# A Fourier filter gated by a ReGLU network: seven block products for a pair of feature tiles in the first 512 rows, four roots by iteration, first turns in halves, and a new order of the program

## The chip, the cores and the metric

The kernel runs on one core of a Trainium2 chip. A core has a matrix engine (TensorE, PE in the profile; its weight loads are listed apart as PEld), a vector engine (VectorE, DVE), a scalar engine for functions of one argument (ScalarE, ACT), a third elementwise engine (GpSimd, POOL), and an engine that here only starts transfers (SyncE, SP). They work at the same time, each on its own queue of instructions in order, and wait for one another by semaphores. The metric is the device time of one run in microseconds. Lower is better.

## The reference

For an input `x` of 2048 rows and 512 columns in 32-bit floats:

```
xn = (x - mean) / sqrt(var + 1e-5)              # each row
X  = rfft2(xn) * (w_r + 1j * w_i)               # over both axes
s  = irfft2(X, (2048, 512))
gate = xn @ W_gate                              # 512 x 1376
up   = xn @ W_up
h    = where(gate > 0, gate, 0) * up
g    = silu(h @ W_down)                         # 1376 x 512
out  = x + s * g
```

So two long chains start from the same normalized rows, a two-dimensional Fourier filter and a gated network, and they meet in the last line.

## The kernel before

**Numbers.** TensorE multiplies 16-bit floats with 32-bit sums. To keep the accuracy each 32-bit matrix is split into a high and a low 16-bit part, and each product is made of three: high by high, high by low, low by high (`PASSES`). Before such a split the weights are scaled by powers of two.

**Rows and features.** The 2048 rows are eight chunks of 256, or four blocks `c` = 0 to 3 of 512 rows, which are four row tiles of 128. The 1376 features are eleven feature tiles `f` = 0 to 10, of which the last has 96. For one block, one feature tile and one of the two matrices a plain product (`product`) is 12 matmuls of 512 columns: four pieces of the 512 input columns, three passes each. Then `rectify` (ScalarE) and `hidden` (VectorE, ScalarE) make the hidden tile `h`; `down` multiplies it by W_down, three matmuls for each feature tile and row tile; `gate` applies silu on ScalarE to the sum of a row tile.

**Seven block products.** For two feature tiles (a pair of `PAIRS`) `fast_products` takes another way, in the manner of Strassen and Winograd: instead of the four plain products of the pair it makes seven block products of 12 matmuls of 256 columns, into the tiles `sa`, `sb` and `sc`, and puts them together with copies and sums on ScalarE and VectorE (`sk`, `se`, `sr`, `sq`). It needs sums and differences of the rows, made by `row_sums` (`sx` on VectorE, ScalarE and POOL, written to memory as `S_d` and read back transposed as `xS`), and sums and differences of the weights, made by `weight_sums` once for each pair (`rp`, `wT`). `fast(c, n)` says whether block `c` uses it for pair `n`: `c >= 4 - int(FASTS[n])`. With `FASTS` at '3' for all five pairs, block 0 makes plain products everywhere and blocks 1 to 3 use the seven products in all pairs.

**The start.** The first 256 rows are loaded, normalized in two tiles `xf`, and turned on TensorE (`turn_row`: `head`, then the copy `xTf` in 32 bits and the 16-bit parts in `xT0`). While the split weights aren't ready, the first two feature tiles are multiplied in 32 bits from `xTf` for the first 256 rows (the matmuls `gu<-xTf,raw`, eight steps of four). Other chunks are turned through memory by SP.

**The normalization of later rows.** `deviations` handles chunks 2 and 3 together, and chunks 4 to 7 together: variance plus epsilon and its reciprocal on VectorE, the square root on ScalarE (line 412), one multiplication on VectorE. The square root and silu are in different function tables of ScalarE, which loads one when it changes from the other. So the silu gates of block 0 read the name "roots", which both calls of `deviations` write (line 961 and after), and come after all square roots.

**The filter.** `first_stage`, `fft_chunk` (eight chunks of frequencies, tiles `xx`, `y`, `z`, `v`, `w`) and `last_stage` (eight chunks of rows, TensorE tile `s`, then `zz`, `ae`, `ye`, `sv`) do the transforms as matmuls with constant matrices. The matmuls of some of these stages run on a part of TensorE's array, a mode of tiling that differs from that of the other products; the last feature tile's narrow product (`gu<-xT,wgt 128*64`) has a mode of its own too.

**The end.** `finish` multiplies the filter's rows by the gate (`sv<-sv,g`) and adds `x`: for chunks 0, 1, 3, 4 and 5 by a transfer on POOL's queue that accumulates onto `x` already copied to the output, for the others by a sum on an engine (`xt<-xt,sv`) and a plain transfer on SP. The last row tile of all is cut into pieces of 256, 128 and 128 columns (`columns`; TensorE's tiles `dn`, `dn_3b`, `dn_3bb`), so that the work behind TensorE's last matmul is short.

**The order.** The program doesn't run its loops as they stand. Each function lists steps in a `Plan` (class at line 176): an engine, what it reads and writes, and a function that makes its instructions. `run` then makes the steps in the sequence `ORDER` (line 68), a tuple of 1606 step numbers; each engine keeps the sequence of its own steps. A step that may run on either of two engines takes the letter in `PLACE` (D, A or P for VectorE, ScalarE or POOL), and a tile takes its buffer from `SLOTS`. So the order of work on every queue is written out by hand, and all instructions carry the line of one helper, L169. Tiles are to be told apart by their names.

Of the kernel before, what the change touches and what calls it, by code (L numbers as in the profile page):

```python
# [15 lines left out]
P = 128  # L16
# [31 lines left out]
BUSY, LATE = 28, 0.4  # L48
SQUARES, HALF = 63.305, 2
# [14 lines left out]
FASTS = ['3', '3', '3', '3', '3']  # L64
# [63 lines left out]
)  # L128
PLACE = (
    "AAPAADAADDAAADADDDADDDAPPDPDDDADDDPDDPAAADAADDDDDPPDPDDDDDDDDDDDDDDPPDADDDAAAADAAADDADDDDPDDDDDDDDDDDDDDDDDDDDPDDDDDDDPPDPPPDPADDDDDDPDDDDDD"  # L130
    "DDDDDDDDDDDDDPDPDDDDDPDDDDDPDPPPDDPDPDDPPPDDDDDPPDPDPPDPDDDDDDPDDDPDDDDDDDDDDDPPDPDDDDPPPDDDDDPPPDDDDPPPDDDPDPDDDDDDDDDDDDDDDDDDDDDDDDDDDDDD"
    "DDDDDDDDDDDDDDDDDDDDDDDDDDDDDDDDDDDDDDDDDDDDDDDDDDDDD"
)
SLOTS = (
# [104 lines left out]
def dve(n):  # L239
    return .07 + n / 960  # L240
# [27 lines left out]
def kernel(ctx: ExitStack, tc: tile.TileContext, x, wg, wu, wd, wl, ew, sp, c_r, c_d, c_m, c_x, c_s, out):  # L268
# [227 lines left out]
    def turn_row(c, i):  # L496
# [6 lines left out]
        elif i == 0:  # L503
            tile_of(name, "F", [P, 2, D], F32)
# [960 lines left out]
```

## Time and profile before

| what | value |
|---|---|
| median of 3 runs | 388.28 us (387.56 to 388.38) |
| the profiled run | 387.25 us, its span 385.4 us |
| TensorE (PE) | 378.9 us busy, 98% of the span, 3525 matmuls |
| VectorE (DVE) | 308.3 us, 80% |
| ScalarE (ACT) | 254.3 us, 66% |
| GpSimd (POOL) | 73.0 us, 19% |
| transfers | 77.95 MB, 202 GB/s on the mean |
| mean granted clock of TensorE | 0.998 of full speed |

The span is the time from the first to the last event of the program in the profile; the run's own time is a little longer. Records of one engine overlap: a matmul of 256 columns has a record of 0.273 us, but twelve of them in a row take 1.31 us. Where a duration of a row of work is wanted, the starts of neighbouring records say more than the mean record. The share of the span in which each engine was busy, in forty slices, in tenths (9 is 90% or more):

```profile
PE   8999999999999999999999999999999999999995
DVE  4999999989769999995369875687368872499996
ACT  4999999899955954666476645664565744386321
POOL 3200102000041200413502132322023033102220
```

TensorE is at 9 in all slices but the first and the last. VectorE is at 9 in the first fifth, in the middle and at the end; ScalarE only in the first quarter.

### The profile page before, as it was taken

How to read it: one execution, taken by the hardware profiler on the slowest of the kernel's cores; microseconds unless marked ns; L12 is line 12 of the kernel's file. 1: busy time of each engine (PE TensorE's matmuls, PEld its weight loads, DVE VectorE, ACT ScalarE, POOL GpSimd, SP SyncE). 2: the span in 40 equal slices, each digit the busy share in tenths (PEclk: the TensorE clock that was granted, in tenths of full speed). 3: DMA queues.
4: the chain of work that ended last, by engine and by line, in shares of the span. 5: the costliest groups of instructions: out<-in, count | busy, mean ns of one | idle time of the engine just before them, and what ended most of it. 6: DMA issues, size and time to landing. Idle time of an engine off the chain costs nothing.

```text
span 385.4 us, 8914 instructions
## 1 busy us (share of the span) xinstructions
PE 378.9 (98%) x3525; PEld 261.7 (68%) x3525; DVE 308.3 (80%) x560; ACT 254.3 (66%) x494; POOL 73.0 (19%) x72
## 2 busy tenths in 40 slices
PE   8999999999999999999999999999999999999995
PEld 6955444444778877646888788755588788778444
DVE  4999999989769999995369875687368872499996
ACT  4999999899955954666476645664565744386321
POOL 3200102000041200413502132322023033102220
PEclk9999999999999999999999999999999999999999
DMA  7989799795369386978858165482676027998997
GB/s 249 404 261 364 206 195 262 229 278 153 109 176 257 115 281 215 261 162 226 269 184 224 60 176 131 107 243 55 196 206 192 2 54 201 225 239 244 226 267 188
DMA packets 67833, 77.95 MB, mean 202 GB/s; under 512 B 29072, under 2 KB 40944, under 8 KB 67792
## 3 DMA queue, kind: packets, MB, share of 16 engines
q1 hardware_dynamic: 66352, 74.77, 67.8%
q0 software_dynamic: 1440, 2.62, 4.4%
q8 instruction: 27, 0.44, 0.5%
q14 instruction: 14, 0.11, 0.1%
HBM read 46.95 MB, written 26.76 MB: 191 GB/s over the span
## 4 chain that ended last, share of the span: by engine, by line
PE 90%; ACT 4%; DVE 3%; DMA 2%; issue 0%; POOL 0%; DVEq 0%
PE dn L169 25%; PE gu L169 17%; PE sb L169 15%; PE sc L169 10%; PE sa L169 10%; PE s L169 3%; PE z L169 3%; PE xx L169 3%; DMA x<-in_x 2%; PE y L169 2%; PE v L169 2%; ACT ju L169 2%; ACT wds L169 1%; DVE xT L169 1%; ACT wT L169 1%; PE dn_3b L169 0%
## 5 line engine op out<-in xcount | busy, mean ns | idle before, releaser
L169 PE MATMUL dn<-wds,h 128*128 128x512 f16 (+2 forms) x528 | 118.9, 372 | 0.0
L169 PEld LDWEIGHTS <-wgu 128*128 128x128 f16 x960 | 92.7, 98 | 36.4 <-issue 1.9
L169 PEld LDWEIGHTS <-h 128*128 128x128 f16 (+1 forms) x594 | 54.4, 98 | 51.4 <-issue 1.8
L169 PEld LDWEIGHTS <-wT 128*128 128x128 f16 x540 | 52.5, 98 | 8.6 <-issue 0.4
L169 PE MATMUL gu<-xT,wgu 128*128 128x512 f16 (+1 forms) x240 | 47.5, 358 | 0.0
L169 PE MATMUL sa<-xT,wgu 128*128 128x256 f16 x360 | 44.3, 273 | 0.0
L169 PE MATMUL sb<-xS,wT 128*128 128x256 f16 x360 | 44.2, 273 | 0.0
L169 PE MATMUL sc<-xS,wgu 128*128 128x256 f16 x180 | 22.1, 273 | 0.2 <-ACT g L169 0.2
L169 PE MATMUL sb<-xS,wgu 128*128 128x256 f16 x180 | 22.1, 273 | 0.0
L169 PE MATMUL sc<-xT,wT 128*128 128x256 f16 x180 | 22.1, 273 | 0.0
L169 DVE TENSOR_TENSOR sc<-sb,sk 128x512 f32<-128x512 f32 x15 | 10.4, 696 | 12.2 <-PE sb L169 9.1
L169 ACT ACTIVATE g<-dn,cdi 128x512 f32<-128x512 f32 (+1 forms) x16 | 10.4, 671 | 11.5 <-PE dn L169 11.5
L169 DVE TENSOR_TENSOR t<-v,t 128x1024 f16<-128x1024 f32 x8 | 9.8, 1222 | 9.4 <-ACT t L169 9.2
L169 POOL TENSOR_TENSOR se<-se,sq 128x512 f32<-128x512 f32 x9 | 11.5, 1273 | 30.2 <-ACT sq L169 30.2
L169 PE MATMUL gu<-xT,wgt 128*64 128x256 f16 (+1 forms) x144 | 17.0, 309 | 0.0
L169 ACT ACTIVATE sq<-sc 128x512 f32<-128x512 f32 x15 | 9.0, 597 | 12.0 <-PE sc L169 7.3
L169 DVE TENSOR_TENSOR h<-gu,r 128x512 f32<-128x512 f32 (+3 forms) x22 | 12.5, 566 | 4.4 <-ACT r L169 2.4
L169 ACT ACTIVATE sb<-sa 128x512 f32<-128x512 f32 x15 | 8.8, 587 | 9.7 <-PE sa L169 8.2
L169 ACT ACTIVATE t<-v 128x1024 f16<-128x1024 f32 x8 | 8.2, 1023 | 10.5 <-PE v L169 10.5
L169 DVE TENSOR_TENSOR w<-xsp,w 128x1024 f32<-128x1024 f32 (+1 forms) x13 | 13.5, 1041 | 1.7 <-ACT w L169 1.3
L169 POOL DMA_DIRECT2D out<-sv x10 | 8.8, 895 | 31.5 <-DVE sv L169 29.3
L169 DVE TENSOR_TENSOR sr<-sb,sr 128x512 f32<-128x512 f32 x15 | 10.3, 685 | 5.4 <-POOL se L169 2.7
(216 smaller groups left out, 721.0 us busy)
## 6 DMA issues: line engine op xcount, KB each, us to landing
rw<-in_wl SPq DMA_DIRECT2D x8, 512.0 KB, 5.5
A_d<-t SPq DMA_DIRECT2D x16, 256.0 KB, 3.5
wt<-in_wl SPq DMA_DIRECT2D x8, 512.0 KB, 5.6
at<-A_d SPq DMA_DIRECT2D x8, 512.0 KB, 5.7
C_d<-t SPq DMA_DIRECT2D x16, 256.0 KB, 3.3
ct<-C_d SPq DMA_DIRECT2D x16, 256.0 KB, 8.1
xf<-in_x SPq DMA_DIRECT2D x6, 512.0 KB, 4.9
N_d<-xf SPq DMA_DIRECT2D x6, 512.0 KB, 3.4
```

Source lines behind the costliest of these rows:

```text
L169: return lambda *args, **kw: self.tc.keep_in_program_order(f(*args, **kw))
```

## The change

1. `FASTS[1]` becomes '4': the pair (3, 4) takes the seven block products in block 0 too. For that `row_sums(0)` runs (two more writes and two more transposed reads on SP), and `weight_sums` of that pair runs before block 0's products. Its plain products, `rectify` and `hidden` of block 0 go.
2. `ITERATE = (4,)`: for chunks 4 to 7 the inverse root is made on VectorE from a first guess by integer arithmetic on the bits and three steps of Newton's iteration, 12 small instructions. The square root on ScalarE goes there, and with it the write of "roots". Chunks 2 and 3 stay as they were.
3. The turns of the first chunk (`head0_0`, `head0_1`), their copies `xTf` and the 32-bit products are done in halves: two transposes, 256 columns, and two matmuls at a time. A `head0` tile is now twice as large, one half for each.
4. `ORDER` (1635 steps), `PLACE` and `SLOTS` are new throughout. Counting the steps, TensorE has 441 (428 before), VectorE 464 (460), ScalarE 434 (426), SP 230 (226) and POOL 66 (66). At the end, the three pieces of the last row tile come in another sequence on TensorE, the 256-wide one last; and `PLACE` gives the last sum of the program (`xt`, that piece's) to POOL.

```diff
+ITERATE = (4,)
...
-FASTS = ['3', '3', '3', '3', '3']
+FASTS = ['3', '4', '3', '3', '3']
...
 ORDER = (
...
 PLACE = (
...
 SLOTS = (
...
-        step("DVE", .38, run, reads=[(st, 2, c, i) for c in cs for i in range(2)], writes=[(q, 0)], port=True)
-        step("ACT", .2, lambda: ACT.activation(y(), v(), AF.Sqrt), reads=[(q, 0)], writes=[(q, 1), "roots"])
-        step("DVE", .19, lambda: DVE.tensor_mul(w(), T[st][:, 1, :], y()), reads=[(q, 1), *((st, 1, c) for c in cs)], writes=[(q, 2)], port=True)
+
+        def iterate():
+            b = T[q].bitcast(I32)
+            DVE.tensor_scalar(w(), T[st][:, 2, :], 64.0 / (D * XS ** 2), EPS * 64.0 / XS ** 2, op0=ALU.mult, op1=ALU.add)
+            DVE.tensor_scalar(b[:, 1, :], b[:, 0, :], -0.5, float(0x5F3759DF), op0=ALU.mult, op1=ALU.add)
+            for k in range(3):
+                DVE.scalar_tensor_tensor(v(), y(), -(4.0 ** -k), y(), op0=ALU.mult, op1=ALU.mult)
+                DVE.tensor_mul(v(), v(), w())
+                DVE.scalar_tensor_tensor(y(), v(), 3.0, y(), op0=ALU.add, op1=ALU.mult)
+            DVE.tensor_mul(w(), T[st][:, 1, :], y())
+        sums_of = [(st, 2, c, i) for c in cs for i in range(2)]
+        if cs[0] in ITERATE:
+            step("DVE", 1.9, iterate, reads=sums_of, writes=[(q, 2)], port=True)
+        else:
...
-        if c == 0:
-            tile_of(name, "F", [P, D], F32)
-        elif i == 0:
+        if c == 0 or i == 0:
             tile_of(name, "F", [P, 2, D], F32)
...
+            def part(a):
+                for k in range(2):
+                    PE.transpose(T[name][:, a, k * P:k * P + P], T[f"xf{c}"][:, i, (2 * a + k) * P:(2 * a + k + 1) * P], unit)
+            for a in range(2):
+                step("PE", .22, lambda a=a: part(a), reads=[(f"xf{c}", i)], writes=[(name, a)], due=HEADS[c])
+            for a in range(2):
+                to = lambda a=a: T[n][:, 2 * a:2 * a + 2].rearrange("p k r -> p (k r)")
+                half = lambda a=a: T[name][:, a, 0:256]
+                T.either([("DVE", dve(256), ...), ("ACT", act(256), ...)], reads=[(name, a)], writes=[(n, a)])
...
-            def whole(j):
-                for k in range(4):
+            def whole(j, a):
+                for k in range(2 * a, 2 * a + 2):
                     matmul(to()[:, j], T[f"raw{g}_{i}"][:, k, :], T[f"xTf{j}"][:, k, :], start=k == 0, stop=k == 3)
...
-            if k > 1 and k % 2 and any(fast(k // 2, n) for n in range(len(PAIRS))):
+            if k % 2 and any(fast(k // 2, n) for n in range(len(PAIRS))):
                 row_sums(k // 2)
...
+    quick = [n for n in range(len(PAIRS)) if fast(0, n)]
     for f in range(HALF, NFT):
+        if any(f in PAIRS[n] for n in quick):
+            continue
...
+    for n in quick:
+        weight_sums(n, TDUE[n])
+        fast_products(0, n)
```

More of the change, by code (lines that the diff above doesn't have):

```diff
@@ L68 @@
 ORDER = (
[59 rows of a table removed]
[61 rows of a table added]
 )
 PLACE = (
-    "AAPAADAADDAAADADDDADDDAPPDPDDDADDDPDDPAAADAADDDDDPPDPDDDDDDDDDDDDDDPPDADDDAAAADAAADDADDDDPDDDDDDDDDDDDDDDDDDDDPDDDDDDDPPDPPPDPADDDDDDPDDDDDD"
-    "DDDDDDDDDDDDDPDPDDDDDPDDDDDPDPPPDDPDPDDPPPDDDDDPPDPDPPDPDDDDDDPDDDPDDDDDDDDDDDPPDPDDDDPPPDDDDDPPPDDDDPPPDDDPDPDDDDDDDDDDDDDDDDDDDDDDDDDDDDDD"
-    "DDDDDDDDDDDDDDDDDDDDDDDDDDDDDDDDDDDDDDDDDDDDDDDDDDDDD"
+    "DDADAAADDADAADAADADDDAAAAPPDDDDDDPDDDDADDDDPPDDAAAAADDADDDDDDDDDDDDDDPADDDDPPDADADDAADAAAADDADDDDPPDDDPDDDDDDDDDDDDDPPADDDDDDDPDPDPDDDADDPPD"
+    "PDDDDDDDDDDDDDDDDDPDDPPDDDDPDDDDDDDDDDDDDPDDDDDPPDPDDDDDPDDDPPDPPPDDDDDPDPDDDDDDDDDDDDDPDPPPDDDDPPPDDDPDDDDDDPPPPPDDDPDPDDDDDDDDDDDDDDDPDDDD"
+    "DDDDDDDPDDDDDDDDDDDPDDDDDDDDDDDDDDDDDDDDDDDDDDDDDDDDDDDDDPDDDD"
 )
 SLOTS = (
-    "00003891323300007162135011720253014206000044921016491487006302918390831448196549051670311501506699616223562219980241411630961259022411185122"
-    "118355963087666020137021820014270591614a0712616053172020422112237076505040213939265842321003128002102303401201206a00210210270213103150709201"
-    "061020130218321031320221002101402011301a52011012791676006052512023100810220121a2102123370012301354021203196074222100050105031418612308120017"
-    "18100661041017212507040603141111190500083508110706021759321618242005037420040717191107751215040608131956031118309032000430614165211041514364"
-    "908398707619212758514201652630376734"
+    "00003891320320000170131631610452056113200075191932782816815130071419574100068800714490180233151055252084185619817646017504695800967422649560"
+    "65194719064917776404002140a25015239070451312820016130712306305324702121037400120307476547162012301a01202102970213203580021101316102302123046"
+    "461704250123210590123201120123103700012313268201230234151a301022610220131521023027620123023902011203022101320a415081130206201016101933251807"
+    "00212311012901171108040806603506072922111920311005141815095637080302041112297811142620011654270611151309057089020761672650522701137130812040"
+    "4434919559808212310057573261064734355407"
 )
@@ L410, in run @@
             DVE.reciprocal(v(), w())
-        step("DVE", .38, run, reads=[(st, 2, c, i) for c in cs for i in range(2)], writes=[(q, 0)], port=True)
-        step("ACT", .2, lambda: ACT.activation(y(), v(), AF.Sqrt), reads=[(q, 0)], writes=[(q, 1), "roots"])
-        step("DVE", .19, lambda: DVE.tensor_mul(w(), T[st][:, 1, :], y()), reads=[(q, 1), *((st, 1, c) for c in cs)], writes=[(q, 2)], port=True)
+        def iterate():
[11 more added lines that the diff above has]
+        else:
+            step("DVE", .38, run, reads=sums_of, writes=[(q, 0)], port=True)
+            step("ACT", .2, lambda: ACT.activation(y(), v(), AF.Sqrt), reads=[(q, 0)], writes=[(q, 1), "roots"])
+            step("DVE", .19, lambda: DVE.tensor_mul(w(), T[st][:, 1, :], y()), reads=[(q, 1), *((st, 1, c) for c in cs)], writes=[(q, 2)], port=True)
         for j, c in enumerate(cs):
@@ L500, in turn_row @@
         name = f"head{c}" + f"_{i}" * (c == 0)
-        if c == 0:
-            tile_of(name, "F", [P, D], F32)
-        elif i == 0:
+        if c == 0 or i == 0:
             tile_of(name, "F", [P, 2, D], F32)
         j = 2 * (c % 2) + i
-        head = lambda: T[name] if c == 0 else T[name][:, i, :]
+        head = lambda: T[name][:, i, :]
         xt = lambda h: T[f"xT{c // 2}"][:, j, 4 * h:4 * h + 4].rearrange("p k r -> p (k r)")
@@ L512, in run @@
                 PE.transpose(head()[:, cols], T[f"xf{c}"][:, i, cols], unit)
-        step("PE", .45, run, reads=[(f"xf{c}", i)], writes=[(name, i)], due=HEADS[c])
-        if c == 0:
+        if c:
+            step("PE", .45, run, reads=[(f"xf{c}", i)], writes=[(name, i)], due=HEADS[c])
+        else:
             n = f"xTf{i}"
             tile_of(n, "k2", [P, 4, P], F32)
-            to = lambda: T[n].rearrange("p k r -> p (k r)")
-            T.either([("DVE", dve(512), lambda: DVE.tensor_copy(to(), head()), False), ("ACT", act(512), lambda: ACT.activation(to(), head(), AF.Copy), False)],
-                     reads=[(name, i)], writes=[n])
+            def part(a):
[6 more added lines that the diff above has]
+                half = lambda a=a: T[name][:, a, 0:256]
+                T.either([("DVE", dve(256), lambda to=to, half=half: DVE.tensor_copy(to(), half()), False), ("ACT", act(256), lambda to=to, half=half: ACT.activation(to(), half(), AF.Copy), False)],
+                         reads=[(name, a)], writes=[(n, a)])
             of = lambda: T[n].rearrange("p k r -> p (k r)")
             T.either([("ACT", act(512), lambda: ACT.activation(xt(0), of(), AF.Copy), False), ("DVE", dve2(512), lambda: DVE.tensor_copy(xt(0), of()), True)],
-                     reads=[n], writes=[(f"xT{c // 2}", j, 0)])
-            both(512, lambda e: e.tensor_sub(xt(1), of(), xt(0)), [n, (f"xT{c // 2}", j, 0)], [(f"xT{c // 2}", j, 1)])
+                     reads=[(n, a) for a in range(2)], writes=[(f"xT{c // 2}", j, 0)])
+            both(512, lambda e: e.tensor_sub(xt(1), of(), xt(0)), [(n, 0), (n, 1), (f"xT{c // 2}", j, 0)], [(f"xT{c // 2}", j, 1)])
             return
@@ L874, in product @@
         if c == 0 and f < HALF and rows.start == 0:
-            def whole(j):
-                for k in range(4):
+            def whole(j, a):
+                for k in range(2 * a, 2 * a + 2):
                     matmul(to()[:, j], T[f"raw{g}_{i}"][:, k, :], T[f"xTf{j}"][:, k, :], start=k == 0, stop=k == 3)
             for j in range(2):
-                step("PE", WHOLE, lambda j=j: whole(j), reads=[f"xTf{j}", f"raw{g}_{i}"], writes=[(name, 0, i)], due=tick(WHOLE))
+                for a in range(2):
+                    step("PE", WHOLE / 2, lambda j=j, a=a: whole(j, a), reads=[(f"xTf{j}", a), f"raw{g}_{i}"], writes=[(name, 0, i)], due=tick(WHOLE / 2))
             sums[c, f, i] = to, [(name, k, i) for k in range(2)]
```

120 rows, old and new, of the table ORDER are left out of this document.

## The prediction, made before the changed kernel was run

> **What bounds the kernel now.** I read the page's totals and its chain first, then the list of what TensorE waited for, then the chain in order of time, and last the timelines of the places that the change touches.
>
> ```profile
> span 385.4 us, 8914 instructions
> PE 378.9 (98%) x3525; PEld 261.7 (68%) x3525; DVE 308.3 (80%) x560; ACT 254.3 (66%) x494; POOL 73.0 (19%) x72
> PE 90%; ACT 4%; DVE 3%; DMA 2%; issue 0%; POOL 0%; DVEq 0%
> ```
> ```profile
> PE small L169 <- DVE md L169: 1.2, 1, 1.2
> PE head L169 <- DVE xf L169: 0.3, 1, 0.3
> PE sum L169 <- DVE xT L169: 0.3, 1, 0.3
> PE gu L169 <- ACT xTf L169: 0.2, 1, 0.2
> PE sc L169 <- ACT g L169: 0.2, 1, 0.2
> ```
>
> The first fence is the page: PE is busy for 98% of the span and is 90% of the chain. The second lists every wait of PE (engine, what it waited for, total, times, longest): five waits, 2.2 us together. So TensorE bounds nearly everything; time comes off only by shorter TensorE work, by one of these waits, or by the stretch after TensorE's last instruction. The profiled run took 387.25 us, 1.85 more than its span; the median of the three runs is 388.28. I work out a difference on the profiled span and add it to the median.
>
> **The seven products.** The chain in order of time (start, us, what):
>
> ```profile
> 335.55 1.31 PE sb L169 x12
> 336.86 0.78 PE s L169 x24
> 337.65 1.42 PE sa L169 x12
> ...
> 343.22 1.44 PE s L169 x48
> ...
> 367.59 5.83 PE dn L169 x27
> ...
> 375.22 4.92 PE dn L169 x39
> ```
> ```profile
> L169 PE MATMUL sa<-xT,wgu 128*128 128x256 f16 x360 | 44.3, 273 | 0.0
> ```
>
> A matmul of 512 columns takes 5.83/27 = 0.216 us, so a plain product of 12 takes 2.59; the 12 half-width ones of a block product take 1.31. Pair (3, 4) for the first 512 rows now takes 4 x 2.59 = 10.36; as seven block products 7 x 1.31 = 9.17. TensorE: **-1.19 us**. Nothing beside TensorE hides this, since it has no wait there.
>
> **Changes of tiling.** The matmuls of the filter stages (tile s) run on a part of the array. One stage of 24 takes 0.78, two together 1.44: entering that mode costs 2 x 0.78 - 1.44 = 0.12. The twelve sa behind a stage take 1.42 where sb takes 1.31: leaving costs 0.11. Counting the steps in the order in which the program makes them, TensorE changes mode 54 times now and 60 times in the new ORDER, because small tail products and filter stages that stood together now stand apart. Six more at 0.115: **+0.69**. Bounds: 0, if they land where TensorE waits anyway, and 1.0: the group of sa has records of 0.273 us at a pitch of 1.31/12 = 0.109, so an array that empties wholly loses 0.164, six times.
>
> The Trainium skill, page "TensorEngine Tiling (Array Packing)", section "Key Properties", speaks against this part of the order: changing the tiling mode, not just the tile, drains the array. The trace agrees that each change costs time (0.11 and 0.12), though less than a whole record's tail; by a full drain each time this term would be the 1.0 in place of 0.69, and the forecast 0.3 later.
>
> **The root by iteration, and the first gates.**
>
> ```profile
> 93.54 0.17 DVE L169 TENSOR_SCALAR q<-st 128x8 f32<-128x8 f32 x1 [0.37 <-ACT ju L169]
> ...
> 94.43 1.28 ACT L169 ACT_TABLE_LOAD   x1
> 95.72 1.84 ACT L169 ACTIVATE g<-dn,cdi 128x512 f32<-128x512 f32 x3
> 96.46 1.47 PE L169 MATMUL sc<-xS,wgu 128*128 128x256 f16 x12 [0.20 <-ACT g L169]
> ```
>
> This timeline shows the root of chunks 4 to 7 holding the first block's gates: after the root ScalarE loads a table (1.28), then the gates free a bank of PSUM, and TensorE stands 0.20 for it. With those chunks' root on VectorE the gates no longer read it: **-0.20**. The gates still read the roots of chunks 2 and 3, which come earlier. VectorE gives nine more small instructions for it, each up to the 0.17 of the first row, at most 1.5 in all; it has that room, since it is 80% busy over the span. If the same gates are late for another reason, the gain is 0; it can't be more than 0.20 where TensorE has no other wait.
>
> **First turns in halves.**
>
> ```profile
> 6.62 1.07 PE L169 MATMUL head<-unit,xf 128*128 128x128 f32 x8 [0.31 <-DVE xf L169]
> 7.94 2.05 PE L169 MATMUL gu<-xTf,raw 128*128 128x128 f32 x16 [0.25 <-ACT xTf L169]
> 8.36 0.69 DVE L169 BATCH_NORM_STATS2 st<-x 128x6 f32<-128x512 f32 x1 [1.42 <-DMA x<-in_x]
> 11.04 0.99 DVE L169 TENSOR_SCALAR xf<-x,mv,q 128x512 f32<-128x512 f32 x2
> 11.72 1.07 PE L169 MATMUL head<-unit,xf 128*128 128x128 f32 x8
> ```
>
> The copy xTf in halves lets TensorE begin its whole products some 0.15 earlier than 7.94. But the second chunk of rows lands only then (VectorE waits for x until 8.36), so its normalized rows come at 11.0 to 12.0 and its turn at 11.7 whatever stands before. TensorE then has nothing else ready and gives the 0.15 back as a wait: **0**, bounds -0.25 (all of that wait) and +0.3 (VectorE takes copies in front of the normalization).
>
> **The earlier row and weight sums.**
>
> ```profile
> 20.00:30.00 10.00, 10.00 (x62) 5.74 (x61) 9.65 (x22) 10.00 (x23) 0.00 (x0) 1.00 0.82 267
> 30.00:40.00 10.00, 10.00 (x87) 5.22 (x85) 9.79 (x22) 9.89 (x27) 0.00 (x0) 1.00 1.07 361
> 50.00:60.00 10.00, 10.00 (x48) 4.48 (x46) 9.55 (x18) 9.21 (x20) 0.00 (x0) 1.00 1.14 187
> ```
> ```profile
> L169 DVE TENSOR_TENSOR sx<-sx,sx 128x1024 f16<-128x1024 f32 x5 | 6.1, 1222 | 0.1
> L169 ACT ACTIVATE sx<-sx 128x1024 f16<-128x1024 f32 x6 | 6.2, 1050 | 3.1 <-DVE wgu L169 2.6 <-DVE sx L169 0.5
> ```
>
> In the windows (stretch, length, then busy time of PE, PEld, DVE, ACT, POOL, the granted clock and the DMA share) VectorE and ScalarE are nearly full up to 60 us, while they split weights for a TensorE that never waits. The seven products of the first block add work exactly there: two more of each 1024-wide instruction of the second fence, one of VectorE's moved to POOL, four 512-wide sums, two more writes of 512 KB and two more transposes behind them on SP. That is some 3.6 us of VectorE and 2.1 of ScalarE into stretches with 0.2 to 0.8 free in ten. TensorE's cover is the distance between a weight's split and its first matmul, which no row shows. I take **+0.3**, the size of the waits in the list above; below, 0, if the order puts the sums behind what is urgent; above, 1.2, one such instruction standing in front of a weight that is due.
>
> **The end.**
>
> ```profile
> 377.54 0.70 DVE L169 TENSOR_TENSOR xt<-xt,sv 128x512 f32<-128x512 f32 x1
> 378.14 0.90 DVE L169 TENSOR_TENSOR sv<-sv,g 128x512 f32<-128x512 f32 x2
> ...
> 379.96 1.17 PE L169 MATMUL dn_3bb<-wds,h 128*128 128x128 f16 x18
> 380.17 0.48 ACT L169 ACTIVATE g<-dn,cdi 128x256 f32<-128x256 f32 x1 [2.92 <-PE dn L169]
> 380.67 0.42 DVE L169 TENSOR_TENSOR sv<-sv,g 128x256 f32<-128x256 f32 x1 [0.23 <-ACT g L169]
> ...
> 381.90 0.29 DVE L169 TENSOR_TENSOR xt<-xt,sv 128x128 f32<-128x128 f32 x1
> ```
> ```profile
> 110.87 0.73 POOL L169 TENSOR_TENSOR xs<-ee 128x256 f32<-128x256 f32 x1
> ```
> ```profile
> out<-xt SPq DMA_DIRECT2D x5, 256.0 KB, 3.8
> ...
> out<-xt SPq DMA_DIRECT2D x2, 64.0 KB, 2.5
> ```
>
> TensorE now ends with 18 narrow matmuls behind the 256-wide piece, at 379.96 + 1.17 = 381.13; the last VectorE sum ends at 382.19, so 1.06 later, and the span ends 3.2 after that. In the new ORDER the narrow pieces come first and the 256-wide one ends the program; and by PLACE its last sum is POOL's. Behind TensorE then stand 0.03 + the 0.48 of ScalarE, 0.02 + the 0.42 of VectorE, a hand-over to POOL (0.2 at most, by the gap of 0.03 to 0.2 between other engines) and POOL's 0.73 for that shape: 1.88 in place of 1.06, **+0.82**. The last transfer is of 128 KB, not 64: between the 2.5 and 3.8 us of the issue rows that is 0 to +0.4; I take **+0.1**, as the span already ends 3.2 behind the last sum.
>
> Whether VectorE keeps up decides the rest:
>
> ```profile
> 345.00:380.00 35.00, 35.00 (x320) 22.06 (x319) 35.00 (x65) 14.11 (x45) 8.80 (x10) 1.00 0.99 236
> ```
>
> VectorE is as full as TensorE for the last 35 us. Counted from the end of the first last stage (337.65 now), the new order leaves TensorE 33 steps of 0.65, 5 of 1.31, 11 of 0.33, 22 of 0.17, seven stages of 0.66 and eleven changes: 41.3 us, so the last gate is ready at 41.8. VectorE has 58 wide instructions (0.60 each, 377.54 to 378.14), 13 of half width at about 0.34 and 4 narrow ones at 0.20 before it, 40.0, behind the 1.2 that it starts later; with the 0.4 by which the same count falls short today, 41.6. A tie: I take **0**, bounds 0 and +1.4 (two wide instructions and their hand-over late).
>
> **Sum.** -1.19 + 0.69 - 0.20 + 0 + 0.3 + 0.82 + 0.1 = **+0.5 us**, so TensorE ends 0.4 earlier and the program 0.5 later. Forecast: **388.8 us**, no measurable change; about 0.2% (0.78 us) is what a measurement of this kernel can tell from none. Its own range is 387.5 to 389.06.
>
> **Rivals.**
>
> Slower, 0.32: VectorE ends the program. Place: the last 41 us; it decides as soon as VectorE loses more than 0.2 us there, since the count above ties. For it: VectorE is full, DMA is at a share of 0.99 in the same stretch, and the loads that VectorE's sums wait for must fit into 2.4 us less of TensorE work (two block products are moved ahead of that stretch). Against it: today it loses only 0.4. Price: one late load of 256 KB is 1 to 1.5 us, with the forecast's 0.5: +1.0 to +2.3, 389.3 to 390.6.
>
> Faster, 0.24: the seven products bring their 1.19 and the order hides the rest: the early sums cost 0, the changes of mode half (0.35), the hand-over to POOL nothing and POOL's sum 0.6, the turns -0.15. -1.19 + 0.35 - 0.20 - 0.15 + 0.5 = -0.7; with all mode changes covered -1.3: 387.0 to 387.5. For it: today's order hides everything but 2.2 us of waits, so one can expect as much of the new one. Against it: POOL's 0.73 is behind everything and nothing can hide it.
>
> The change doesn't do what it says (0.05 of the 0.32 above): the sums of the first rows come too late, TensorE waits for their transposes in the seven products and loses the 1.19 there: +0.5 + 1.19 = +1.7, 390.0. For it: four more instructions and two transposes on full engines; against it: the seven products stand near the end of the first block's products, when most weights are split.
>
> **Numbers.** No change 0.44, faster 0.24, slower 0.32. Cutting about one in ten on each side gives the range 387.0 to 390.6, which covers the unknown early waits, the tie at the end and the two bounds of the changes of mode.
>
> **What would show it.** Right: 84 block-product matmuls more and 48 wide ones fewer in the groups of sa, sb, sc and gu; the wait of sc for g gone; TensorE's last instruction at about 380.7; POOL's xt as the last sum, about 1.9 after it. Wrong: waits of TensorE of over 0.5 us between 16 and 62 us (the early sums cost more); VectorE busy until after the last gate is ready (the tie lost); TensorE ending before 380 (the changes of mode cost less, or other waits went); the last sum within 1.2 of TensorE's end (POOL's sum is cheaper than its row).

## The result, and the profile after

The changed kernel takes 389.82 us (median of 4 runs, 389.66 to 391.05); the kernel before, run beside it, 388.11 (387.56 to 388.38). The ratio is 1.0057, with a 95% interval of 1.0042 to 1.0073: slower by 2.2 us (1.6 to 2.8). The two medians lie only 1.7 apart; the ratio takes in all runs, the one of 391.05 among them. That is inside the range of the prediction, but not its likeliest case; it is the place of the slower rival. The profiled run took 389.92 us, 2.67 more than that of before.

The totals on the page of the changed kernel, and one of its groups:

```profile
span 388.1 us, 9006 instructions
...
PE 379.0 (98%) x3561; PEld 265.0 (68%) x3561; DVE 315.6 (81%) x574; ACT 259.5 (67%) x502; POOL 71.6 (18%) x72
...
L172 PE MATMUL sa<-xT,wgu 128*128 128x256 f16 x384 | 47.2, 273 | 0.0
...
L172 PE MATMUL gu<-xT,wgu 128*128 128x512 f16 (+1 forms) x192 | 37.0, 352 | 0.0
```

The work is what the change says: 24 more matmuls in `sa` alone (84 in its five groups together) and 48 fewer wide ones in `gu`. TensorE's busy time is the same (379.0, before 378.9), though less work was given to it; VectorE's grew by 7.3 us. The list of TensorE's waits after the change:

```profile
PE head L172 <- DVE xf L172: 1.3, 1, 1.3
PE small L172 <- DVE md L172: 1.2, 1, 1.2
```

`sc` for `g`, 0.2 before, is gone as forecast, and so are `sum` for `xT` and `gu` for `xTf`; `head` for `xf` went from 0.3 to 1.3. And the timeline of the end:

```profile
381.26 1.89 DVE L172 TENSOR_TENSOR xt<-xt,sv 128x512 f32<-128x512 f32 x3
381.94 0.47 ACT L172 ACTIVATE g<-dn,cdi 128x256 f32<-128x256 f32 x1 [2.92 <-PE dn L172]
383.07 0.41 DVE L172 TENSOR_TENSOR sv<-sv,g 128x256 f32<-128x256 f32 x1
383.58 0.72 POOL L172 TENSOR_TENSOR xt<-xt,sv 128x256 f32<-128x256 f32 x1 [4.75 <-DVE sv L172]
```

TensorE's last matmul ends at 381.91. The gate `g` is ready at 382.41, but VectorE is in three older sums until 383.15 and takes the gate's product only then (its records overlap by some hundredths); POOL's sum ends at 384.30, 2.39 behind TensorE, where the last sum of before was 1.06 behind it. The span ends 6.2 after TensorE, before 4.27.

**Where the 2.7 us went.** A list of waits shows too little here: TensorE's short stalls of 0.1 to 0.3 us lie inside groups of records. I therefore cut the run at instructions that both programs have, by the starts of TensorE's records (us: from the first turn `head` to the first plain product of 512 columns; to the first filter stage `xx`; to the first `v`; to the first last stage `s`; to the last one; to TensorE's end):

```
kernel          head->512  ->xx     ->v     ->s      ->last s  ->end
before          12.749     180.414  19.904  117.100  18.601    25.742
changed         16.365     179.702  20.556  116.684  19.663    22.290
a_modes2        16.560     179.684  20.555  116.707  19.431    22.293
b_halves        13.076     180.402  19.904  117.100  18.598    25.743
b_iterate       13.669     180.301  19.904  117.100  18.598    25.743
```

Read the columns, not the rows: from the first 512-wide product on, two runs with the same order agree to about 0.02 us. Only the first column and what lies behind the last sum vary between runs. In the first column the changed kernel has 24 matmuls of 256 columns done that the other still has to do, 24 x 0.109 = 2.62. The four parts of the difference in span:

```
start, equal work, apart from x's landing    16.365-12.749-2.62-0.82   +0.18
x's second chunk lands (VectorE's first work on it, 9.18 against 8.36)   +0.82
TensorE from there to its end                358.90 - (361.76-2.62)    -0.25
behind TensorE's end                         6.24 - 4.27               +1.97
                                                                 sum   +2.7
```

The columns behind the first sum to 361.76 in the kernel before and to 358.90 in the changed one. So in these two profiles most of the loss, 1.97 of 2.7, stands behind TensorE's last matmul, and the pair's gain is nearly used up before it. Of the 1.97, 1.33 is the later last sum (2.39 behind TensorE, before 1.06); the other 0.64 comes behind the last sum, in a stretch that takes 3.0 to 4.2 us in the profiles of the changed kernel and its variants and 2.9 to 4.1 in those of the kernel before and its variants.

### The profile page after: what moved, and what is told of

Read it like the earlier page. It is cut to its first block, busy times and chain, and to the rows that moved or that the text cites. A ratio compares the mean times of both kernels' runs of the same rounds, so it can differ in the third digit from the quotient of the medians.

```text
span 388.1 us, 9006 instructions
## 1 busy us (share of the span) xinstructions
PE 379.0 (98%) x3561; PEld 265.0 (68%) x3561; DVE 315.6 (81%) x574; ACT 259.5 (67%) x502; POOL 71.6 (18%) x72
## 3 DMA queue, kind: packets, MB, share of 16 engines
q0 software_dynamic: 1440, 2.62, 4.2%
## 5 line engine op out<-in xcount | busy, mean ns | idle before, releaser
L172 PEld LDWEIGHTS <-wT 128*128 128x128 f16 x576 | 56.0, 98 | 9.5 <-issue 0.6
L172 PE MATMUL sa<-xT,wgu 128*128 128x256 f16 x384 | 47.2, 273 | 0.0
L172 PE MATMUL sb<-xS,wT 128*128 128x256 f16 x384 | 47.2, 273 | 0.0
L172 PE MATMUL gu<-xT,wgu 128*128 128x512 f16 (+1 forms) x192 | 37.0, 352 | 0.0
L172 PE MATMUL sc<-xS,wgu 128*128 128x256 f16 x192 | 23.6, 273 | 0.1
L172 DVE TENSOR_TENSOR se<-sb,sk 128x512 f32<-128x512 f32 x16 | 11.0, 688 | 7.6 <-PE sb L172 6.0
L172 ACT ACTIVATE a<-y 128x1024 f16<-128x1024 f32 x8 | 8.1, 1022 | 13.4 <-PE y L172 13.4
L172 ACT ACTIVATE z<-z 128x1024 f16<-128x1024 f32 x8 | 8.2, 1023 | 11.0 <-PE z L172 11.0
L172 ACT ACTIVATE sr<-sa 128x512 f32<-128x512 f32 x16 | 9.4, 590 | 7.7 <-PE sa L172 7.7
L172 DVE TENSOR_TENSOR z<-z,z 128x1024 f16<-128x1024 f32 x8 | 9.8, 1222 | 5.7 <-ACT z L172 5.7
```

Source lines behind the costliest of these rows:

```text
L172: return lambda *args, **kw: self.tc.keep_in_program_order(f(*args, **kw))
```

## The experiments

Two theories stood against one another at the start of the experiments. The first: the loss is at the end, because the 256-wide piece is last and VectorE, not TensorE, ends the program. The second: the loss is at the start, where two small loads (`s`, 8 KB, and `edge`, 32 KB, steps 482 and 481) were moved in front of the weights on SP's queue and hold up `x`. Names that begin with a are the changed kernel with an edit, those with b the kernel before. Each ratio is to the kernel before, run beside it. The changed kernel itself has only its own four runs, so ratios that differ from its 1.0057 by 0.1% can't be told from it.

**The two small loads.**

```diff
 # a_loads_back, ORDER
-35, 36, 482, 21, 22, ... 57, 56, 481, 41, 43, ... 70, 141, 84, 142, 145,
+35, 36, 21, 22, ... 57, 56, 41, 43, ... 70, 141, 84, 482, 481, 142, 145,
```

> The changed kernel, with the two small loads of the filter's edge and scale (32 KB and 8 KB in short pieces), which its order puts ahead of the second 256 rows of x on SP, put back behind ten of the first weight loads. Nothing else is moved. My theory: these two made x land 0.9 us later (9.15 us in place of 8.26), TensorE waited 1.30 for the second rows and is 1.0 late at 23 us for it. Then here x lands at 8.2 to 8.5, the wait of head for xf is 0.3 to 0.6, and the time falls by 0.6 to 1.0 us, to about 389.0. Rival: the late landing is chance of a run or comes from the other loads' order; then x lands at 9.0 to 9.3 still and the time stays at 389.8 within 0.3.

389.06 us, ratio 1.0032 [1.0020, 1.0043]. The start of its timeline:

```profile
8.79 0.69 DVE L172 BATCH_NORM_STATS2 st<-x 128x6 f32<-128x512 f32 x1 [0.76 <-DMA x<-in_x]
...
12.18 0.63 PE L172 MATMUL head<-unit,xf 128*128 128x128 f32 x4 [0.93 <-DVE xf L172]
```

The second chunk of x was there 0.39 us sooner than in the changed kernel's profile, where the same two rows are:

```profile
9.18 0.69 DVE L172 BATCH_NORM_STATS2 st<-x 128x6 f32<-128x512 f32 x1 [1.14 <-DMA x<-in_x]
...
12.56 0.63 PE L172 MATMUL head<-unit,xf 128*128 128x128 f32 x4 [1.30 <-DVE xf L172]
```

At the end the last sum stands 2.05 behind TensorE, 0.34 nearer than in the changed kernel: VectorE's list of waits there lacks the 0.3 for `sv` that the changed kernel's has. The opposite edit is the test:

```diff
 # b_loads_early, ORDER: the same two loads (467, 468 there) up to where the changed kernel has them
+34, 33, 468, 35, 51, ... 40, 39, 467, 43, 41, ...
-415, 627, 467, 513, 628, ... 515, 420, 468, 553, 190,
```

> The kernel before, with the same two small loads moved to where the changed kernel has them: one behind the first rows of x, one right ahead of the second rows. My theory: the second rows land about 0.9 us later than 8.26, TensorE waits that much longer for them, and the kernel takes 0.5 to 1.0 us more, 388.6 to 389.1. Rival (the loads are no matter, the halves of the first turns or the order of the weights' splits make the start late): x lands at 8.3 and the time is that of before within 0.3.

388.29 us, ratio 1.0016 [1.0007, 1.0026] (one run of eleven, of 1399 us, is left out). In its profile x is late:

```profile
9.42 0.69 DVE L169 BATCH_NORM_STATS2 st<-x 128x6 f32<-128x512 f32 x1 [2.46 <-DMA x<-in_x]
```

Taken alone the two runs speak for the second theory: 0.25% back, 0.16% lost. But the landing of the same rows in all profiled runs (us) doesn't keep to it:

```
loads late:   before 8.36, b_halves 8.47, b_less_dma 9.02, b_iterate 9.71, a_loads_back 8.79
loads early:  changed 9.18, b_loads_early 9.42, a_sc 8.14, a_modes 8.47, a_tail 8.76, a_sum_dve 8.79, a_modes2 9.02, a_less_dma 9.57, a_no_pair 8.91
```

The means are 8.87 and 8.92, and each row of the list spans some 1.4 us. One profile of each kernel thus can't carry the theory; whether the loads are worth the 0.16 to 0.25% that the timed runs show stays open. What is settled is what a late landing does: it goes to the end of the program one for one. From the landing to the first 512-wide product it takes 11.01 or 11.02 us in every profile of the kernel before and its variants, and 13.84 in those of the changed kernel (13.94 in a_tail and 14.41 in a_sum_dve), and everything behind is rigid.

**The last sum.**

```diff
 # a_sum_dve, PLACE, the last sum of the program
-P
+D
```

> The changed kernel with one letter of PLACE changed: the last sum of the program (xt, 256 columns) is VectorE's in place of POOL's. My theory: POOL's hand-over and 0.72 become about 0.45 on VectorE, so the last sum ends 0.3 to 0.4 earlier and so does the program: 389.4 to 389.5. Rival: the last transfers (the accumulations on POOL's queue end at 384.1, beside the last sum at 384.3) set the end; then the last sum ends earlier and the time stays at 389.8 within 0.15.

389.76 us, ratio 1.0054 [1.0041, 1.0066], against 1.0057 [1.0042, 1.0073] with POOL. The end of its timeline:

```profile
383.27 0.42 DVE L170 TENSOR_TENSOR sv<-sv,g 128x256 f32<-128x256 f32 x1
383.73 0.43 DVE L170 TENSOR_TENSOR xt<-xt,sv 128x256 f32<-128x256 f32 x1
```

The last sum ends 2.05 behind TensorE instead of 2.39: POOL's slower sum is 0.34 of the tail, as its rows say (0.72 against 0.43, and a hand-over). In the time that isn't resolved. VectorE is as late as before: the gate was ready at 382.14 + 0.47 = 382.61, and its product starts 0.66 after that. So POOL's sum is a part of the loss, but not the tie that was lost.

**VectorE's queue at the end.** In the last 44 us the changed kernel's VectorE begins with `sc`, and this row of the timeline shows what for:

```profile
342.33 0.70 DVE L172 TENSOR_TENSOR sc<-sb,sk 128x512 f32<-128x512 f32 x1 [2.22 <-ACT ye L172]
```

2.22 us idle, then a sum of 0.70, in front of the first sums of the last stages. Edit: that step (1112) behind three of those.

```diff
 # a_sc, ORDER
-1503, 1504, 1112, 1492, 1496, 1443, ... 1498, 1499, 1548,
+1503, 1504, 1492, 1496, 1443, ... 1498, 1499, 1112, 1548,
```

> The changed kernel with one step of VectorE moved: the sum sc of the last pair, for which VectorE idles 2.2 us at 340 to 342.3 while the filter rows' first sums already could be made, comes behind three of these. My theory: this idle time is what makes VectorE 0.66 late at the end, so VectorE gets 0.3 to 0.5 of it back and the time falls by 0.2 to 0.5. Rival: the later sc holds a bank that TensorE needs and TensorE waits; then its list of waits grows by 0.5 to 1.5 and the time rises.

389.48 us, ratio 1.0045 [1.0032, 1.0059]. The end, and VectorE's waits from 338 to 384 us:

```profile
380.90 0.47 ACT L172 ACTIVATE g<-dn,cdi 128x256 f32<-128x256 f32 x1 [2.92 <-PE dn L172]
381.81 0.42 DVE L172 TENSOR_TENSOR sv<-sv,g 128x256 f32<-128x256 f32 x1
382.31 0.72 POOL L172 TENSOR_TENSOR xt<-xt,sv 128x256 f32<-128x256 f32 x1 [4.41 <-DVE sv L172]
```
```profile
DVE ae L172 <- ACT zz L172: 1.9, 1, 1.9
...
DVE ye L172 <- POOL ae L172: 0.6, 1, 0.6
```

The gate is ready at 381.37 and VectorE comes 0.44 later, 0.66 in the changed kernel. That isn't the moved sum's doing: this run, like a_loads_back, lacks the wait of 0.3 for `sv` that the changed kernel has. In a_loads_back, where `sc` stands as in the changed kernel, the last sum ends 2.05 behind TensorE; here it ends 2.16 behind. So the move cost 0.11: VectorE begins with `ae` sooner, but then stands 0.6 for POOL's half of it. The ratio can't be told from the changed kernel's. The edit doesn't show that `sc` is what makes VectorE late, nor that it isn't; it exchanged one idle time for another.

**Two sums exchanged.** The 512-wide sum that stands in VectorE's way at the end to POOL, an earlier one and the last to VectorE.

```diff
 # a_tail, PLACE
-P  (last sum, 256 wide)      D  (xt of chunk 6's first row tile, 512 wide)
+D                            P
```

> The changed kernel with two letters of PLACE changed: the last sum (xt, 256 columns) goes from POOL to VectorE, and one of the three 512-wide sums that VectorE makes right ahead of the last gate's product goes to POOL, which is idle then. My theory: VectorE's lateness (0.66 behind the last gate) and POOL's hand-over both go; the last sum ends 1.3 to 1.6 behind TensorE in place of 2.40, and the time falls by 0.6 to 1.0. Rival: the last transfers, which queue behind POOL's accumulations until 384.1, set the end; then the sum ends earlier and the time falls by less than 0.3.

390.43 us, ratio 1.0076 [1.0062, 1.0090]: no gain. Timeline:

```profile
379.23 1.39 POOL L170 TENSOR_TENSOR xt<-xt,sv 128x512 f32<-128x512 f32 x1 [0.73 <-DVE sv L170]
379.42 1.75 DVE L170 TENSOR_TENSOR sv<-sv,g 128x512 f32<-128x512 f32 x1
...
381.30 0.68 DVE L170 TENSOR_TENSOR sv<-sv,g 128x512 f32<-128x512 f32 x1
```

The same VectorE instruction takes 0.68 alone and 1.75 beside POOL's sum: it ends at 381.17, 0.55 after POOL's. What VectorE saved by the exchange it lost by standing beside POOL, and the last sum came 2.51 behind TensorE. The Trainium skill, page "SBUF — State Buffer", section "SBUF: two separate sides", says why an idle POOL is no free helper: VectorE and GpSimd share a pair of ports under an exclusive lock, and the later one fully blocks. These two rows agree with it.

**Changes of tiling mode.** In the changed kernel some steps in a mode of their own stand alone that could stand side by side.

```diff
 # a_modes2, ORDER: v next to y; a narrow gu next to v; the s of one chunk next to the next one's
-1288, 1013, ... 1091, 1128, 1089, ... 1481, 1460, 1477,
+1310, 1288, 1327, ... 1410, 1128, 1074, ... 1475, 1460, 1503,
```

> As a_modes, but without the step that delayed the narrow product of the first rows (it made TensorE wait 1.3 us for a bank): three steps moved, 56 changes of mode in place of 60. My theory: 0.12 us each, so TensorE ends 0.45 to 0.55 earlier against its first turn than in the changed kernel (375.26 from the first turn to the last matmul's end, so 374.7 to 374.8), if the second rows of x land at the same time, and the time falls by 0.2 to 0.5. Rival: a change costs nothing on the sum; then that stretch is 375.2 to 375.4.

389.60 us, ratio 1.0063 [1.0039, 1.0087]: no gain. At their places all three moves paid: two filter stages `s` side by side 0.23 (19.663 to 19.431 in the segments above), the two neighbours of different modes 0.10 each (`v` beside `y` takes 1.68, apart 0.88 and 0.91). But the segment of those two came out 0.02 longer, because TensorE has a new stall of 0.24 there, between `dn` and `z` at 273.3 us, that the changed kernel doesn't have. And the 0.23 didn't reach the end. From the start of the first last stage TensorE needs 41.72 us here and 41.95 in the changed kernel; the last sum ends 44.35 after that point here and 44.34 there. That is the clearest sign of who ends the program: TensorE gained 0.23 in the last 42 us, and the last sum, which waits for VectorE, did not move. The other arrangement, with one more narrow product moved (564, from behind 87 to behind 120), was slower:

> The changed kernel with four steps of TensorE moved so that stages in a mode of tiling stand together as in the kernel before: 55 changes of mode in place of 60. My theory: a change costs 0.12 us wherever it stands, so TensorE ends 0.6 earlier, and with VectorE 0.65 late at the end the program gains 0 to 0.6: 389.2 to 389.8; in the trace TensorE's last instruction comes 0.5 to 0.7 earlier against its start. Rival: the changes cost nothing on the sum, since TensorE then waits elsewhere; then TensorE ends at 381.9 as now and the list of its waits grows by 0.6.

390.72 us, ratio 1.0083 [1.0069, 1.0097]. The list of TensorE's waits has a new row:

```profile
PE sum L172 <- DVE h L172: 1.3, 1, 1.3
```

a_modes2, without the moved narrow product, doesn't have this wait, so the run measures its own edit there. At the end it shows the same as a_modes2: TensorE needs 41.72 us from the first last stage, and the last sum ends 44.34 after it.

**The transfers.** The DMA share is at 1.0 at the end, so the end could also be the transfers'. The ten accumulating transfers were cut to a quarter, in both kernels.

```diff
-POOL.dma_start(to, T[sn][:, i, :], accum_op=ALU.add)
+POOL.dma_start(to[:, 0:128], T[sn][:, i, 0:128], accum_op=ALU.add)
```

> The changed kernel with the ten accumulating transfers of the end cut to the first 128 of their 512 columns (the other columns of these rows are left at x); every instruction of the engines stays. My new theory: from 9 us behind the last v stage the DMA engines are full to the end (share 1.03 to 1.13), so the program ends when their work is done and not when TensorE, VectorE or POOL are; at TensorE's end 3.8 us of DMA work are left, against 2.1 in the kernel before. With 5 to 10 us of that work gone the last write lands 1.5 to 2 behind the last sum, VectorE isn't late any more, and the time falls by 1.0 to 2.0 us, to 387.8 to 388.8. Rival: VectorE's lateness and POOL's last sum set the end; then the last sum still comes 2.4 behind TensorE and the time falls by less than 0.5.

> The kernel before with the same cut of the accumulating transfers. My new theory: its DMA engines have 1.6 us of slack some 28 us ahead of TensorE's end and 2.1 us of work left there, so less hangs on them: the time falls by 0.3 to 0.8 us, clearly less than in the changed kernel. Rival: less work of that kind is worth the same in both, so it says nothing of the change; then both fall by the same within 0.3.

a_less_dma: 389.63 us, ratio 1.0048 [1.0032, 1.0064]. b_less_dma: 387.25 us, 0.9987 [0.9978, 0.9995]. The same stretch in the windows (stretch, length, busy time of PE, PEld, DVE, ACT, POOL, clock, DMA share, GB/s) of the changed kernel, and then of a_less_dma:

```profile
360.00:380.00 20.00, 20.00 (x105) 9.94 (x104) 19.75 (x38) 6.43 (x24) 6.93 (x8) 1.00 1.01 237
```
```profile
360.00:380.00 20.00, 20.00 (x113) 9.72 (x102) 19.74 (x38) 6.71 (x24) 6.92 (x8) 1.00 0.70 171
```

With the share down to 0.70, VectorE is as full as it was (19.74 of 20), and the last sum still ends 2.39 behind TensorE (384.68 - 382.29). Both kernels gain half a microsecond at most (the changed one 0.35 by its two ratios, whose intervals overlap; the one before 0.5); the difference between them stays. So a crowded queue is not what makes VectorE late. None of VectorE's waits in that stretch names a load either, and that part of the slower rival falls.

**The pair alone.** `FASTS[1]` back to '3' in the new order, with the plain products put where the seven block products stood.

```diff
-FASTS = ['3', '4', '3', '3', '3']
+FASTS = ['3', '3', '3', '3', '3']
```

> The changed kernel with FASTS back at '3' for the pair (3, 4): in the first 512 rows the two tiles are four plain products again, where the seven block products stood; the sums of these rows and their transposes are left out, and the steps that overwrite the two tiles' split weights come behind the products. The rest of the order stands. My theory: TensorE has no wait that the sums cause, so the pair is worth its 1.19 us in full; here TensorE ends 1.0 to 1.3 later against its first turn, and the time rises by 0.8 to 1.4 us to 390.6 to 391.2. Rival: the early sums on VectorE and ScalarE eat the gain (the waits of 0.30 at 62 us and 0.31 at 107 us are theirs); then both are gone here and the time rises by 0.6 or less.

402.19 us, ratio 1.0381 [1.0361, 1.0401]. The list of its waits begins:

```profile
PE dn L165 <- DVE h L165: 4.5, 1, 4.5
PE sb L165 <- ACT sb L165: 3.3, 1, 3.3
```

These two waits are neither kernel's; they come from the plain products standing in an order made without them. The run tells nothing of what the pair is worth. It does tell of one of the two small stalls that its rival names, the one at 107 us:

```profile
119.99 1.47 PE L165 MATMUL sa<-xT,wgu 128*128 128x256 f16 x12
...
121.59 1.47 PE L165 MATMUL sc<-xS,wgu 128*128 128x256 f16 x12
```

Twelve such matmuls take 1.31, so `sc` could begin at 121.30, and it begins 0.29 late, nearly as in the changed kernel (0.31). With the pair's early sums left out the stall stands, so they don't make it. At the other place TensorE stands 0.37 here, but behind work that this edit delays; that one stays without a test.

**The root and the halves, each alone in the kernel before.**

```diff
 # b_iterate: ITERATE = (4,) and iterate() of the change, nothing else
 # b_halves: part(a), to(a), half(a), whole(j, a) of the change, nothing else
```

> The kernel before with the root by iteration for chunks 4 to 7 and nothing else: one step of VectorE where two steps and ScalarE's root stood. My theory: the gates no longer wait for the table, TensorE's wait of 0.20 for g at 96 us goes and nothing is late instead, so the last v stage comes 0.2 earlier and the time falls by 0.1 to 0.3. Rival: the 12 small instructions hold up the weights' work on VectorE and another wait of 0.1 to 0.4 takes its place; then the time stays.

> The kernel before with the first turns, copies and 32-bit products in halves and nothing else, each half right behind the other where the whole step stood (the first copy on VectorE, the second on ScalarE). My theory: TensorE begins the products 0.1 to 0.2 earlier and gives it back to the wait for the second rows, so the start costs nothing: from the first turn to the first 512-wide product 12.7 to 12.9 us as before if x lands at the same time, and the time stays within 0.3. Rival: the halves' copies hold up VectorE's normalization, and the start is 0.3 to 0.5 longer whenever x lands.

b_iterate: 388.37 us, ratio 1.0019 [1.0007, 1.0031]. Its waits of TensorE, and the root in its timeline:

```profile
PE small L164 <- DVE md L164: 1.2, 1, 1.2
PE head L164 <- DVE xf L164: 0.8, 1, 0.8
PE sum L164 <- DVE xT L164: 0.3, 1, 0.3
PE gu L164 <- ACT xTf L164: 0.2, 1, 0.2
```
```profile
94.88 0.17 DVE L164 TENSOR_SCALAR q<-st 128x8 f32<-128x8 f32 x1 [0.36 <-ACT ju L164]
...
95.66 1.28 ACT L164 ACT_TABLE_LOAD   x1
...
96.13 1.48 PE L164 MATMUL sa<-xT,wgu 128*128 128x256 f16 x12
...
96.96 1.84 ACT L164 ACTIVATE g<-dn,cdi 128x512 f32<-128x512 f32 x3
...
97.69 1.47 PE L164 MATMUL sc<-xS,wgu 128*128 128x256 f16 x12
```

The table load runs beside the iteration, and the list no longer has a wait of `sc` for `g`. But the starts show that the stall is smaller and not gone. `sc` could begin at 96.13 + 1.31 = 97.44; it begins 0.25 late, right behind the first of the three gates, which ends at 97.64. In the kernel before the row in front of `sc` is this:

```profile
94.79 1.48 PE L169 MATMUL sa<-xT,wgu 128*128 128x256 f16 x12
```

There `sc` could begin at 96.10 and begins at 96.46, 0.36 late. So the edit takes 0.11 off: the root leaves ScalarE, but the load of the table, 1.28, still stands in front of the gates. The segment up to `xx` says the same (180.301 against 180.414). The time doesn't show it: it reads 0.19% more. In its profiled run x landed at 9.71, 1.35 later than in that of before, and the first column of the segments is 0.92 longer. Its other eleven runs have no profile, and why the mean of them should be late, when nothing at the start was edited, no run here shows.

b_halves: 387.98 us, ratio 1.0009 [0.9997, 1.0021]. From the normalization of the second rows to the first 512-wide product it takes 8.336 us, in the kernel before 8.338. What TensorE gains by beginning earlier it gives back there.

## Why the prediction was right or wrong, step by step

The range (387.0 to 390.6) held, the sign of the sum was right, and the likeliest case wasn't. Term by term:

- **The seven products, -1.19: right.** 48 matmuls of 0.216 fewer and 84 of 0.109 more are -1.21.
- **Changes of mode, +0.69: right, a little too large.** The starts of TensorE's records show an excursion from the full array and back to cost 0.23 more than its matmuls (`s` alone 0.89 for 0.66; two together 1.55, so one excursion saved). Summed over the 29 excursions now and 24 before they take 0.62 us more, where six changes at 0.115 were forecast. Two steps in different modes side by side still pay for one change between them (0.10), two in the same mode pay nothing. On the page "TensorEngine Tiling (Array Packing)" of the Trainium skill, section "Key Properties", a change of mode drains the array; the trace agrees that every change costs, also from one partial mode to another, at 0.10 to 0.12 and not the 0.164 of a whole record's tail that I held against it.
- **The root, -0.20: the stall goes, and another comes.** By the starts the stall in front of `sc` was 0.36, not the 0.20 of the list, and in the changed kernel no `sc` stands for a gate any more; b_iterate shows that the root alone is worth 0.11 of it. What the term had at nothing is a wait for VectorE:

```profile
106.16 0.17 DVE L172 TENSOR_SCALAR q<-st 128x8 f32<-128x8 f32 x1 [0.30 <-ACT ju L172]
...
107.58 1.47 PE L172 MATMUL sa<-xT,wgu 128*128 128x256 f16 x12
...
108.46 0.69 DVE L172 TENSOR_TENSOR sr<-sb,sr 128x512 f32<-128x512 f32 x1
...
109.20 1.47 PE L172 MATMUL sc<-xS,wgu 128*128 128x256 f16 x12
```

  The twelve small instructions hold VectorE's queue from 106.16 to 108.55. `sr`, whose `sb` TensorE has finished at 107.74, comes behind them, and `sc` begins as `sr` ends, at 109.20 in place of 107.58 + 1.31 = 108.89: 0.31 late. The stall is there in a_no_pair too. That the iteration makes it is read from these rows; no run takes the iteration out of the changed kernel. Both stalls together are -0.05.
- **Halves, 0: right.** b_halves shows exactly the giving back that was forecast; in the changed kernel the start costs 0.18, inside the bounds.
- **Early sums, +0.3: near, but not by the mechanism named.** Two more stalls are new, 0.30 at 62 us and 0.115 at 101 us (behind ScalarE's copy of `sa`), 0.41 together. The first:

```profile
60.47 1.47 PE L172 MATMUL sa<-xT,wgu 128*128 128x256 f16 x12
61.14 0.70 DVE L172 TENSOR_TENSOR sc<-sb,sk 128x512 f32<-128x512 f32 x1
...
61.75 0.28 DVE L172 TENSOR_SCALAR wide_md<-unit,md 128x128 bf16<-128x128 f32 x1
...
62.08 0.23 PE L172 MATMUL rows_md<-wide_md,ones 128*128 128x128 bf16 x1
```

  TensorE could go on at 61.78 and waits 0.30 for `wide_md`. In the kernel before `wide_md` follows right behind the reduction that it reads; here a sum that puts the pair's products together, `sc`, stands between the two. So this wait comes with the pair, but from its last sums and not from the sums of rows and weights that the term was for. It is read from the rows and not tested. The prediction named as a sign waits of over 0.5 us between 16 and 62 us; there are none.
- So TensorE from equal work on: -1.21 + 0.62 - 0.05 + 0.41 = -0.23, and the segments give -0.25. This sum was forecast as -0.4 (-1.19 + 0.69 - 0.20 + 0.3). **What TensorE does was read well enough; the failure is behind its end.**
- **The end, +0.82: nearly right.** The chain behind TensorE, without VectorE's lateness, is 0.50 to the gate, 0.51 to POOL's start and POOL's 0.72: 1.73, where 1.88 was forecast, so +0.67. The hand-over to POOL costs 0.1, not 0.2.
- **"A tie: I take 0": this is the step that failed.** I counted 41.8 us from the end of the first last stage to the last gate and 41.6 for VectorE. The gate came after 41.67 and VectorE after 42.33, 0.66 late. The number of VectorE's instructions was right (58 wide, 13 of half width, 4 narrow), and so was their time (40.35 without the two waits below, 40.4 counted with the shortfall). Two things weren't. I let VectorE begin 1.2 us behind that stage, as the kernel before does with `ae`. In the new order its first instruction is `sc`, which needs a product that TensorE makes behind that same stage (340.74 to 342.22), and it begins after 1.59: 0.39. And I had no idle time in the stretch; there is 0.13 in front of the first `ye` and 0.26 in front of an `sv`:

```profile
DVE sv L172 <- DVE sv L172: 0.3, 1, 0.3
```

  These 0.78 use up the 0.2 that the count left, and the gate came 0.13 sooner than counted. What ends the wait of `sv` stays open: the instruction named had ended 0.24 us before. a_loads_back, a_sc and a_no_pair lack this wait, and VectorE is 0.3 to 0.4 late there. The condition that I gave the slower rival (VectorE loses more than 0.2 us) was met; its price, a late load, was wrong, as a_less_dma and VectorE's list of waits show. a_modes2 and a_modes show the rival's core: TensorE faster by 0.23, the last sum no earlier.
- **The last transfer, +0.1: not told from the spread.** Behind the last sum the span goes on for 3.85 us in the changed kernel's profile and for 3.21 in that of before, +0.64. But the same stretch takes 3.0 to 4.2 us in the eight profiles of the changed kernel and its variants that make all transfers (mean 3.70), and 3.2 to 4.1 in four of the kernel before (mean 3.56). The means differ by 0.14, near what was forecast, within a spread of 1.1.
- **Not in the prediction:** the landing of x, +0.82 between the two profiled runs. It is no work of the change that could be shown; with other runs the same programs land it anywhere from 8.1 to 9.7 us. Without it the profile's difference is 1.9 us, within the interval of the timed runs (1.6 to 2.8).

So between the 0.5 us of the forecast and the 1.9 of the profile stand the lost tie, 0.66; the stretch behind the last sum, 0.54; the start, 0.18; the root with its new stall, 0.15; the early stalls, 0.11; POOL's chain, -0.15; the modes, -0.07; the products, -0.02: +1.4 together. What repeats from profile to profile is less: the start, TensorE, the last sum and the mean behind it give 0.18 - 0.25 + 1.33 + 0.14 = 1.4 us of loss, a little under the 1.6 to 2.8 of the timed runs. What makes up the rest is open. No version run here beats the kernel before beyond its interval with the whole work done.

## What to carry to other kernels

When two engines are both full to the end, shortening one moves the end only by as much as the other's queue allows: list the queue of each from the last common point, with its first instruction and what that one waits for, and call a tie a loss. Compare two programs from points of equal work by instruction starts; stretches that repeat to 0.02 us let terms of 0.1 us be read from a single profile, apart from a start and a stretch behind the last sum that each vary by half of the whole effect or more. A list of waits is not the list of stalls: compare the pitch of the starts with what the row of work takes. A sum given to an idle POOL can cost VectorE more than it saves, so look at what VectorE does in the same microsecond.

## What the runs showed of the hardware that was not expected

- A VectorE sum of two operands in SBUF stretches from 0.68 to 1.75 us beside a POOL sum that began 0.19 earlier, and ends 0.55 after it (a_tail). In the changed kernel, too, one is hit, this one in the middle of the run, while the sum in front of it keeps its 0.68 (it reads `sb` from PSUM, but it also began before POOL's sum, so these rows don't tell which of the two spares it):

```profile
119.79 0.68 DVE L172 TENSOR_TENSOR sr<-sb,sr 128x512 f32<-128x512 f32 x1
120.39 1.52 DVE L172 TENSOR_TENSOR h<-se,h 128x512 f16<-128x512 f32 x1
```
```profile
120.09 1.27 POOL L172 TENSOR_TENSOR rp<-rp 128x512 f32<-128x512 f32 x1 [6.07 <-DVE rp L172]
```

- The landing of x's second chunk varies over 1.35 us (8.36 to 9.71) between before, b_halves and b_iterate, whose loads at the start are the same in the same order, and it passes to the end undiminished.
- A change between two partial modes of tiling costs as much as one between a partial mode and the full array: a step of `v` and one of `y` alone take 0.88 and 0.91, next to one another 1.68, so only one change of four, 0.10, is saved.
